# Attention plus mixture of experts on one core: one head pair turned on TensorE in fp32, and softmax inverse sums taken in pairs

## The chip, the cores and the metric

The kernel runs on one core of a Trainium2 chip, as one launch. The metric is the device time in microseconds (us) from start to end of the launch; lower is better. The engines are PE (matrix multiply, with PEld for its weight loads), DVE (vector), ACT (activation functions), POOL (GpSimd) and SP, whose queue here issues transfers and transposing transfers. Each engine takes its own instructions strictly in the order in which the program wrote them.

## The reference

Attention with rotary embedding over 4 batches, 8 heads, 576 positions and 64 dimensions, in fp32, then a layer of 8 experts that is applied densely with weights balanced by 8 Sinkhorn rounds:

```python
scores = (1 / np.sqrt(D)) * np.matmul(q_rot, k_rot.transpose(0, 1, 3, 2))
scores = scores - np.max(scores, axis=-1, keepdims=True)
attn = np.exp(scores)
attn = attn / (np.sum(attn, axis=-1, keepdims=True) + 1e-09)
x = np.matmul(attn, v)                  # regrouped to 2304 tokens x 512
P = np.exp(x @ w_gate - (x @ w_gate).max())
for _ in range(8):
    P /= P.sum(1, keepdims=True) + 1e-09
    P /= P.sum(0, keepdims=True) + 1e-09
    P *= N / E
for e in range(E):
    out += P[:, e:e + 1] * (np.maximum(x @ w1[e], 0.0) @ w2[e])
```

## The kernel before, in words

The 32 heads are taken as 16 pairs (p = 0 to 15, four to a batch). One pair needs 9 tiles of 128 queries: four per head, and one (u = 4) that holds 64 queries of each head. The tiles are numbered m = 9p + u. The steps of a tile, with the names that the order uses and the lines of the profile:

- `S`: scores on PE, an fp32 product (`s_mm`, L528). One S writes the tiles of both heads into a PSUM buffer; the program has three such double buffers (NS = 3).
- `M`: the row maximum, negated, on DVE (`m_max`, L532).
- `ex`: the exponential on ACT with its row sum (`e_exp`, L539). For u = 0, 2, 5, 7 it goes to an fp32 tile in SBUF, otherwise back into PSUM.
- `ei`: two DVE instructions on a 128x1 column, the sum plus 1e-9 (L545) and the reciprocal (L553), one pair of them for each tile.
- `eh`: exponential times inverse sum, rounded to fp16, on ACT (`e_hi`, L556). `el`: the rest, exponential times inverse sum minus eh, also as fp16, on DVE (`e_lo`, recorded at L414). For u = 7 ACT normalises (L559) and POOL subtracts (L563).
- `TR`: the tile's fp16 pair, 128x1152, is turned by a transposing transfer on the SP queue (`e_turn`, L605; u = 4 takes two).
- `AV`: the product with v on PE in fp16 (`av_mm`, L646): three terms, high and low part of v with the high part of the weights and the high part of v with the low part. v is split by `vh` (ACT, L418), `vl` (DVE, L414) and `vb` (DVE, L511).
- `h0, l0, h1, l1`: the result of each half of the queries to fp16 high and low parts of x (`x_half`, ACT L656, DVE L658).

Pairs 0 and 1 of a batch go one after the other. Pairs 2 and 3 of a batch are a group that shares the buffer of turned weights half by half (`GROUPS`, `split`), so their AV products come in column pieces of 256 and 32.

Beside the attention run the preparation of expert 0's weights (`wm`, `wz`, `wh`, `wl`) and, once x of enough pairs is there, its first product (`F1`, L783, three matmuls of 256 columns to a step), its evacuations (`Fh` on ACT L789, `Fl` on DVE L793), its second product (`F2`, L802) and the copies of its output (`Fo`, L807). After the last pair come the logits (`lm`, L668 and L673, and `le`, L681), the gate with its Sinkhorn rounds (`gate`, from L1021), sums of x for the experts to come (`xs`, L1100 to L1116 on DVE; `xp` on PE, L1140), the weights of the next half expert, and the scaling of expert 0's output (L1058). Then a second plan runs the remaining experts; its matmuls are all at L1312.

What comes when, up to the experts, is written out by hand: the string `ORDER` lists every step by name, and the program emits the instructions of all engines in that order. Semaphores are derived from the data and the buffers. So a step that waits holds up all that stands behind it on its engine.

```python
def e_inv(b):
    if not EIP:
        e_eps(b)
    t = b.pop()
    b.append(small.tile([P, 1], F32, tag="ei", bufs=12, name="ei"))
    dve.reciprocal(b[3], t)
```

Of the kernel before, what the change touches and what calls it, by code (L numbers as in the profile page):

```python
# [18 lines left out]
P = 128  # L19
# [12 lines left out]
GROUPS = tuple(g for b in range(4) for g in ((4 * b,), (4 * b + 1,), (4 * b + 2, 4 * b + 3)))  # L32
# [21 lines left out]
FLIP = ()  # L54
EIP = False
# [18 lines left out]
    PT=1.3, pa=0.75, pb=0.6,  # L74
# [16 lines left out]
et0.0 et1.0 ldv.0.0 ld.1 ldv.0.1 ly.1 w.1.0 w.2.0 ldv.0.2 w.1.1 ld.3 w.1.2 ldv.0.3 cq.1 ck.1 S.0.0 sq.1 M.0 v0.0  # L91
ex.0 aq.1 M.1 S.1.0 wm.1.0 ex.1 sk.1 ei.0 ei.1 ak.1 eh.0 v1.0 eh.1 M.3 M.2 ex.3 el.1 ex.2 el.0 ck.3 S.2.0 ei.2 TR.0
ei.3 eh.2 M.4 eh.3 el.2 ly.3 ex.4 el.3 ei.4 S.3.0 TR.3 wm.1.1 eh.4 el.4 M.5 TR.2 v2.0 sq.3 ex.5 M.6 S.4.0 ei.5 sk.3
ex.6 v3.0 eh.5 ld.2 M.7 ak.3 TR.1 ei.6 ex.7 vg.0 M.8 tt.v0 eh.6 ei.7 tm.v0 el.5 ex.8 ta.v0 el.6 vs.0 ck.2 S.5.0 TR.6
wm.1.2 vp.0 cq.3 w.1.3 ei.8 vh.0 M.10 TR.4 eh.7 vb1.0 M.9 eh.8 ex.9 el.8 ex.10 vl.0 S.6.0 TR.8 en.7 ei.10 ei.9 vb0.0
el.7 eh.9 TR.5 M.11 eh.10 M.12 ex.11 cq.2 el.10 TR.7 ex.12 wm.1.3 S.7.0 aq.3 ei.11 gx M.13 tt.g eh.11 AV.0.0.0 ly.2
ei.12 AV.0.0.1 ex.13 tm.g AV.0.0.2 AV.0.0.3 eh.12 ei.13 AV.0.0.4 el.11 ta.g eh.13 et0.1 TR.10 el.12 h0.0 gs S.8.0
TR.12 el.9 sk.2 l0.0 el.13 TR.9 M.14 sq.2 wx.1 wm.2.0 ex.14 tt.w1 AV.0.1.0 TR.11 AV.0.1.1 vh.1 aq.2 AV.0.1.2 M.15
S.9.0 ei.14 ex.15 vl.1 ak.2 eh.14 AV.0.1.3 ei.15 ld.4 M.16 AV.0.1.4 eh.15 et1.1 TR.13 M.17 ex.16 el.15 ex.17 ei.16
S.10.0 el.14 eh.16 tm.w1 en.16 w.2.1 ei.17 ta.w1 M.18 TR.14 eh.17 el.16 M.19 ex.18 el.17 ex.19 ei.18 S.11.0 vb1.1  # L100
eh.18 ei.19 TR.15 vb0.1 ws.1 eh.19 M.20 AV.1.0.0 wz.1.0 vh.2 AV.1.0.1 M.21 TR.17 AV.1.0.2 ex.20 AV.1.0.3 el.19
AV.1.0.4 wz.1.1 ex.21 et0.2 ei.20 S.12.0 ei.21 TR.16 eh.20 el.18 wz.1.2 eh.21 M.22 wh.1.0 TR.19 h1.0 el.21 ex.22
# [241 lines left out]
def attention_moe(ctx, tc, qk, v, trigs, eye, wg, w1, w2, out):  # L344
# [1305 lines left out]
```

## Time and profile before

| | us |
|---|---|
| three runs | 1641.42, 1639.41, 1638.05 |
| their median | 1639.41 |
| the profiled execution | 1643.98 |
| span of its trace, first to last instruction | 1642.2 |
| PE busy in the span | 1568.2 (95%) |
| DVE busy | 1378.7 (84%) |
| ACT busy | 1067.1 (65%) |
| POOL busy | 570.0 (35%) |

A sum over the trace is a sum against the profiled execution, which lies 1.78 us above its span and 4.57 us above the median. A busy PE includes the time in which the last columns of a matmul run out. PEclk, where it is printed, is the clock that TensorE was granted, as a share of 2.4 GHz; it knows two levels, 2.4 and 1.2 GHz, and a number between them is a mean over a stretch.

### The profile page before, as it was taken

How to read it: one execution, taken by the hardware profiler on the slowest of the kernel's cores; microseconds unless marked ns; L12 is line 12 of the kernel's file. 1: busy time of each engine (PE TensorE's matmuls, PEld its weight loads, DVE VectorE, ACT ScalarE, POOL GpSimd, SP SyncE). 2: the span in 40 equal slices, each digit the busy share in tenths (PEclk: the TensorE clock that was granted, in tenths of full speed). 3: DMA queues.
4: the chain of work that ended last, by engine and by line, in shares of the span. 5: the costliest groups of instructions: out<-in, count | busy, mean ns of one | idle time of the engine just before them, and what ended most of it. 6: DMA issues, size and time to landing. Idle time of an engine off the chain costs nothing.

```text
span 1642.2 us, 36750 instructions
## 1 busy us (share of the span) xinstructions
PE 1568.2 (95%) x14682; PEld 1305.4 (79%) x14682; DVE 1378.7 (84%) x2793; ACT 1067.1 (65%) x2192; POOL 570.0 (35%) x472
## 2 busy tenths in 40 slices
PE   4779999999889999999999999999999999999998
PEld 2446565666658989898989898989898989898987
DVE  7899898987869888888888888888888888888777
ACT  4778777874366766666666666666666666666642
POOL 4587444523123333333233323332333323232310
PEclk9879999999999999999999999999999999999999
DMA  8898999984224556565646464646464646464533
GB/s 255 166 195 174 191 189 204 184 141 107 78 102 123 149 129 156 126 158 124 160 121 163 119 165 116 167 114 170 112 171 111 168 116 163 121 161 123 133 100 97
DMA packets 226427, 238.99 MB, mean 146 GB/s; under 512 B 177360, under 2 KB 177488, under 8 KB 222672
## 3 DMA queue, kind: packets, MB, share of 16 engines
q1 hardware_dynamic: 207536, 175.30, 39.7%
q0 software_dynamic: 18720, 61.35, 20.9%
q8 instruction: 115, 1.88, 0.5%
q14 instruction: 56, 0.46, 0.1%
HBM read 123.36 MB, written 9.44 MB: 81 GB/s over the span
## 4 chain that ended last, share of the span: by engine, by line
PE 71%; DVE 4%; ACT 2%; issue 1%; DMA 0%; POOLq 0%; DVEq 0%; SPq 0%; ACTq 0%
PE m L1312 68%; PE g L783 1%; PE g L802 1%; ACT accA L1058 0%; PE g L646 0%; DMA wraw<-in_w 0%; DVE ts L1091 0%; DVE wmx L411 0%; DVE w1l L414 0%; DVE m L1104 0%; DVE hl L793 0%; DVE cs L1041 0%; DVE m L1100 0%; DVE ts L1149 0%; DVE w2l L414 0%
## 5 line engine op out<-in xcount | busy, mean ns | idle before, releaser
L1312 PE MATMUL m<-w2h,h 128*128 128x256 f16 x3528 | 627.2, 273 | 3.3 <-DVE accB L1375 1.5
L1312 PEld LDWEIGHTS <-h 128*128 128x128 f16 x5292 | 515.3, 98 | 63.5 <-issue 2.0
L1312 PE MATMUL m<-w2l,h 128*128 128x256 f16 x1764 | 480.8, 273 | 0.0
L1312 PEld LDWEIGHTS <-w1h 128*128 128x128 f16 x3920 | 369.2, 98 | 40.4 <-issue 3.7
L1312 PE MATMUL m<-ts,w1h 128*128 128x256 f16 (+1 forms) x2240 | 347.6, 262 | 1.9 <-ACT u L1335 1.3
L1377 ACT ACTIVATE ev<-m,pp 128x256 f32<-128x256 f32 x468 | 198.0, 469 | 186.1 <-PE m L1312 185.1
L1312 PE MATMUL m<-ts,w1l 128*128 128x256 f16 (+1 forms) x1120 | 284.0, 262 | 0.0
L1312 PE MATMUL m<-xx,w1h 128*128 128x256 f16 (+1 forms) x1680 | 261.4, 262 | 1.2 <-ACT accB L807 1.2
L1262 POOL TENSOR_TENSOR wraw<-wraw 128x512 f32<-128x512 f32 x112 | 159.2, 1421 | 185.0 <-issue 149.8
L1312 PE MATMUL m<-xx,w1l 128*128 128x256 f16 (+1 forms) x840 | 213.1, 262 | 0.0
L1312 PEld LDWEIGHTS <-w1l 128*128 128x128 f16 x1960 | 191.8, 98 | 17.7
L1357 POOL TENSOR_TENSOR h<-u,h 128x512 f16<-128x512 f32 (+1 forms) x70 | 78.2, 1117 | 362.1 <-ACT h L1353 362.1
L1375 DVE SCALAR_TENSOR_TENSOR ev<-m,pp,ev 128x256 f32<-128x256 f32 x351 | 154.8, 478 | 45.4 <-ACT ev L1377 28.3
L528 PE MATMUL s<-raw 64*128 64x288 f32 (+1 forms) x640 | 126.2, 480 | 39.8 <-DVE et L414 14.3
L1353 ACT ACTIVATE h<-m 128x512 f16<-128x512 f32 (+1 forms) x210 | 120.6, 574 | 44.1 <-PE m L1312 40.7
L1338 DVE TENSOR_TENSOR u<-m,u 128x512 f32<-128x512 f32 (+1 forms) x140 | 88.9, 635 | 55.0 <-PE m L1312 29.2
L528 PEld LDWEIGHTS s<-raw 64*128 64x128 f32 (+1 forms) x640 | 67.2, 197 | 83.9 <-issue 33.2
L1353 ACT ACTIVATE h<-u 128x512 f16<-128x512 f32 (+1 forms) x210 | 122.5, 587 | 14.8 <-DVE u L1364 11.1
L1335 ACT COPY u<-m 128x512 f32<-128x512 f32 (+1 forms) x140 | 76.0, 543 | 71.3 <-PE m L1312 70.3
L481 POOL TENSOR_TENSOR raw<-raw,trig 128x576 f32<-128x576 f32 x60 | 88.5, 1490 | 82.0 <-DMA raw<-in_qk 80.1
L532 DVE TENSOR_REDUCE nm<-s 128x1 f32<-128x576 f32 x144 | 105.4, 748 | 11.2 <-PE s L528 10.7
L1385 POOL DMA_DIRECT2D accA<-ev x78 | 69.2, 1021 | 126.4 <-ACT ev L1377 108.3
(159 smaller groups left out, 2735.7 us busy)
## 6 DMA issues: line engine op xcount, KB each, us to landing
ts<-xd SPq DMA_DIRECT2D x110, 512.0 KB, 3.9
accA<-ev POOLq DMA_DIRECT2D x78, 512.0 KB, 6.1
wraw<-in_w SPq DMA_DIRECT2D x28, 1024.0 KB, 4.9
raw<-in_qk SPq DMA_DIRECT2D x32, 576.0 KB, 4.7
accB<-ev POOLq DMA_DIRECT2D x26, 512.0 KB, 6.8
ts<-xd SPq DMA_DIRECT2D x28, 256.0 KB, 3.0
accB<-ev POOLq DMA_DIRECT2D x26, 256.0 KB, 3.3
vraw<-in_v SPq DMA_DIRECT2D x16, 320.0 KB, 5.0
```

Of the source, the lines that this page charges most:

```text
L481: engine[e].tensor_tensor(x, x, trig[:, n, :], op=ALU.mult)
L528: pe.matmul(o, q, x[r, 1, QH[kh]], start=True, stop=True)
L532: dve.tensor_reduce(b[0], ps[:, :, 0:HS], axis=AX.XY, op=ALU.max, negate=True)
L1262: put(k, "pool", US["ptt"], lambda: pool.tensor_tensor(quad(o), quad(x), quad(y), op=op), deps, uses=[raw])
L1312: pe.matmul(live[bank][:, f_ * width : (f_ + 1) * width], step(x, i, f_), y[:, i], start=first and f_ == 0 and n == 0, stop=n == 5, skip_g ...
L1335: act.copy(live[n], live[src])
L1338: dve.tensor_tensor(live[n], live[x], live[n], **add)
L1353: act.activation(t[:, 0:cols], live[src], func)
L1357: engine[eng].tensor_tensor(l, live[src], h, **sub)
L1375: dve.scalar_tensor_tensor(o, x, s, o, op0=ALU.mult, op1=ALU.add)
L1377: act.activation(o, x, AF.Copy, scale=s)
L1385: pool.dma_start(out=accs(th * NT2 + t0_, nt), in_=ev[th][:, 0:nt], accum_op=ALU.add)
```

## The change

Three things are done.

**Inverse sums in pairs.** The two tiles of one S write their row sums into the two columns of one 128x2 tile, and the two DVE instructions of `ei` run once for both, after both exponentials. The tail tile (u = 4) still has its own.

**Pair 3 by another way** (`WHOLE = (3,)`). Its exponentials stay whole in fp32, in SBUF tiles borrowed from the pool of expert 0's hidden layer (`e_whole`). ACT makes a 128x128 diagonal of each tile's inverse sums (`dg`, `e_diag`). PE multiplies the exponentials, as weights, with that diagonal in fp32, which turns and normalises them at once into a PSUM buffer of the scores' kind (`PT`, `e_flip`). ACT copies the result into storage inside x that is not yet in use (`tc`, `e_copy`), and the product with v runs in fp32 on the unsplit v. So pair 3 has no `eh`, `el`, `TR`, `vh`, `vl` and `vb`. Pair 2 stands alone, and its AV products come in pieces of 288 columns.

**The order.** The string is written anew, the part after the last pair too. The steps of pair 3 stand between those of pairs 1 and 2. One unused cast of the identity at the start (`idf`, L1537) is gone, and unused functions for turning fp16 on PE.

```diff
-GROUPS = tuple(g for b in range(4) for g in ((4 * b,), (4 * b + 1,), (4 * b + 2, 4 * b + 3)))
+WHOLE = (3,)
+GROUPS = ((0,), (1,), (2,)) + tuple(g for b in range(1, 4) for g in ((4 * b,), (4 * b + 1,), (4 * b + 2, 4 * b + 3)))
+ND = 3
...
+    turned = xx.bitcast(F32).rearrange("p a c h n -> p (a c) h n")
+    last64 = att.tile([P, S], F32, name="last64")
...
+    def e_inv(two, n):
+        t, r = (small.tile([P, n], F32, tag=x, bufs=k, name=x) for x, k in (("et", 8), ("ei", 12)))
+        dve.tensor_scalar(t, two[0], 1e-9, 2.0**-N_TOP, op0=ALU.add, op1=ALU.mult)
+        dve.reciprocal(r, t)
+        two.append(r)
...
+    def e_whole(ps, b, n, two, j, k):
+        if not two:
+            two.append(small.tile([P, k], F32, tag="es", bufs=8, name="es"))
+        t = ("hh", "hl")[n % 2]
+        b += [two, hA.tile([P, 2048], F16, tag=t, bufs=2, name=t)[:, 0 : 2 * S].bitcast(F32), j]
+        act.activation(b[2].rearrange("p (a b) -> p a b", a=2), ps[:, :, 0:HS], AF.Exp, bias=b[0], accum_out=two[0][:, j : j + 1])
+
+    def e_diag(b):
+        b.append(att.tile([P, P], F32, tag="dg", bufs=ND, name="dg"))
+        act.activation(b[4], ident, AF.Copy, scale=inv(b))
+
+    def e_flip(bs, j):
+        t = ps_s.tile([P, 2, 512], F32, tag="s", name="s").rearrange("p a b -> p (a b)")
+        bs[j].append(t)
+        mm = lambda *x: pe.matmul(*x, start=True, stop=True)
+        x, d = bs[j][2], bs[j][4]
...
+        for k in range(4):
+            mm(t[:, k * P : k * P + P], x[:, k * P : k * P + P], d)
+        for h, r in enumerate(HEADS if j else ()):
+            mm(t[r, 512:640], bs[h][2][:, 512:576], bs[h][4])
+
+    def e_copy(n, bs, j):
...
+        copy(turned[:, 4 * j : 4 * j + 4, h, HS + q : HS + q + P], t[:, 0:512].rearrange("p (k w) -> p k w", k=4))
+        if j:
+            copy(last64[:, QT[i] : QT[i] + P], t[:, 512:640])
...
     def av_mm(p, qh, jt):
...
+        if p in WHOLE:
+            b, c = divmod(p, KC)
+            for j, r in enumerate(HEADS):
+                k, y = (slice(0, P), turned[:, 4 * j + jt, qh, HS:]) if jt < 4 else (r, last64[r, QH[qh]])
+                pe.matmul(po[r], vraw[b][k, c, j, jt, :], y, start=jt == 0, stop=jt == 4)
+            return
```

Where the instructions move, by engine. First DVE from the first row maximum of pair 0: `L532` and, in the changed kernel, `L531` is M, `L411` and `L406` are maxima of v and of weights, `L414` and `L409` is el. Before:

```order
L532 TENSOR_REDUCE nm<-s 128x1
L411 TENSOR_REDUCE wmx<-wraw 128x1
L545 TENSOR_SCALAR et<-es 128x1
L553 RECIPROCAL ei<-et 128x1
L545 TENSOR_SCALAR et<-es 128x1
L553 RECIPROCAL ei<-et 128x1
L411 TENSOR_REDUCE vmx<-vraw 128x1
L532 TENSOR_REDUCE nm<-s 128x1 x2
```

And now:

```order
L531 TENSOR_REDUCE nm<-s 128x1 x2
L406 TENSOR_REDUCE wmx<-wraw 128x1
L543 TENSOR_SCALAR et<-es 128x2
L544 RECIPROCAL ei<-et 128x2
L406 TENSOR_REDUCE vmx<-vraw 128x1
L531 TENSOR_REDUCE nm<-s 128x1 x2
```

Four small instructions between two pairs of maxima became two, on two columns.

Then PE in the middle of pair 3, between scores of pairs 2, 3 and 4: `L527` is S, `L564` is PT (an x4 row is four fp32 products; the rows of 64 are the last 64 positions), `L659` is AV of pair 3 in fp32, `L857` and `L864` are the turn of a maximum of weights. All rows but S are new:

```order
L564 MATMUL s<-dg,hh 128x128 x4
L564 MATMUL s<-dg,hl 128x128 x4
L564 MATMUL s<-dg,hh 64x128
L564 MATMUL s<-dg,hl 64x128
L527 MATMUL s<-raw 128x288 x4
L659 MATMUL g<-xx,vraw 64x288 x4
L659 MATMUL g<-last_106,vraw 64x288 x2
L564 MATMUL s<-dg,hl 128x128 x4
L564 MATMUL s<-dg,hh 64x128
L564 MATMUL s<-dg,hl 64x128
L564 MATMUL s<-dg,hh 128x128 x4
```

The fp32 products of pair 3 stand between scores, and each group of PT rows takes one of the PSUM buffers of the scores; before, the products of pair 3 with v stood later, in pieces of 256 and 32 columns, and no product turned anything.

Last DVE behind the last logits (`L681`, `L682` and now `L706`, `L707`): `L1100` to `L1116` and now `L1137` are sums of x, `L793` and `L818` is Fl, `L1021`, `L1022` and now `L1058`, `L1059` open the gate. Before:

```order
L681 COPY lg<-g 128x2x24
L682 TENSOR_TENSOR lg<-g,lg 128x2x24
L1100 TENSOR_TENSOR m_5505<-xx 128x512
L1104 TENSOR_TENSOR m_5505<-m_5505,c_5506 128x512
L1106 TENSOR_TENSOR u_5507<-xx,m_5505 128x512
L793 SCALAR_TENSOR_TENSOR hl<-g,hh 128x256
L1109 TENSOR_TENSOR u_5507<-u_5507,xx 128x512
L1091 TENSOR_TENSOR ts<-m_5505,ts 128x512
L1112 TENSOR_TENSOR u_5508<-xx,u_5507 128x512
L1116 TENSOR_TENSOR u_5508<-u_5508,xx 128x512
L1091 TENSOR_TENSOR ts<-u_5507,ts 128x512
L793 SCALAR_TENSOR_TENSOR hl<-g,hh 128x256
```

And now:

```order
L706 COPY lg<-g 128x2x24
L707 TENSOR_TENSOR lg<-g,lg 128x2x24
L1058 TENSOR_SCALAR lg<-lg,inv 128x144
L1059 TENSOR_TENSOR lg<-lg,ctok 128x144
L1061 TENSOR_REDUCE gmx<-lg 128x1
L818 SCALAR_TENSOR_TENSOR hl<-g,hh 128x256
L1137 TENSOR_TENSOR m_5057<-xx 128x512
L818 SCALAR_TENSOR_TENSOR hl<-g,hh 128x256
```

The gate, which stood behind a block's sums of x and two Fl, now opens directly behind the logits. Behind that place stand 86 steps of F1 where there were 70, and 22 of Fl where there were 18; the 56 steps of F2 are the same.

## Rows read from the trace of the kernel before

**Rows 1.** Windows: us, busy PE, PEld, DVE, ACT, POOL, clock, DMA share.

```profile
0.00:20.00 20.00, 5.53 (x16) 3.02 (x16) 12.23 (x19) 4.15 (x8) 9.42 (x12) 1.00 0.79 286
20.00:110.00 90.00, 62.25 (x384) 36.74 (x384) 81.01 (x185) 62.88 (x128) 56.19 (x40) 0.81 0.89 195
110.00:200.00 90.00, 82.69 (x783) 54.47 (x782) 80.39 (x185) 69.71 (x153) 62.16 (x44) 0.96 0.87 177
200.00:300.00 100.00, 97.24 (x924) 61.61 (x924) 88.59 (x211) 77.35 (x166) 49.55 (x35) 1.00 1.01 199
300.00:391.00 91.00, 88.58 (x959) 62.03 (x956) 70.57 (x175) 65.14 (x142) 25.14 (x20) 1.00 0.89 153
391.00:498.00 107.00, 93.05 (x626) 60.55 (x625) 86.48 (x182) 52.31 (x104) 28.88 (x22) 1.00 0.23 84
498.00:1642.00 1144.00, 1138.92 (x11002) 1026.95 (x11002) 959.47 (x1842) 735.60 (x1495) 338.71 (x303) 1.00 0.54 137
```

**Rows 2.** Chain that ended last, in order of time: start, us, what.

```profile
360.50 0.17 DVE et L545
...
360.77 1.40 DVE nm L532 x2
...
378.65 2.08 PE g L646 x56
...
390.88 0.22 DVE lg L681
...
400.96 1.11 DVE lg L1021
...
475.21 4.90 ACT accA L1058 x8
...
497.93 1116.11 PE m L1312 x10756
```

**Rows 3.** Waits of PE, 0 to 200 us: engine, line, releaser, us, times, longest.

```profile
PE s L528 <- DVE et L414: 13.7, 7, 3.6
...
PE s L528 <- ACT e L539: 10.2, 8, 1.9
```

**Rows 4.** DVE and ACT groups, 0 to 500 us: busy, mean ns, idle before.

```profile
L414 DVE SCALAR_TENSOR_TENSOR et<-s,ei,et 128x576 f16<-128x576 f32 x80 | 65.0, 812 | 10.2 <-ACT et L556 9.7
L556 ACT ACTIVATE et<-s,ei 128x576 f16<-128x576 f32 x80 | 58.7, 736 | 15.9 <-DVE ei L553 10.3 <-ACT s L539 2.6 <-issue 1.3
...
L414 DVE SCALAR_TENSOR_TENSOR et<-e,ei,et 128x576 f16<-128x576 f32 x48 | 48.3, 1006 | 1.6 <-ACT et L556 1.6
...
L553 DVE RECIPROCAL ei<-et 128x1 f32<-128x1 f32 x144 | 23.6, 164 | 4.9
...
L545 DVE TENSOR_SCALAR et<-es 128x1 f32<-128x1 f32 x144 | 21.1, 146 | 10.8 <-ACT s L539 7.9 <-ACT e L539 2.3
...
L414 DVE SCALAR_TENSOR_TENSOR vl<-vraw,s,vh 128x640 f16<-128x640 f32 x16 | 14.7, 920 | 0.0
...
L511 DVE COPY vb<-vh 64x512 f16<-64x512 f16 x32 | 12.3, 385 | 0.9
...
L1146 ACT CAST ts<-x 128x256 f16<-128x256 f32 x4 | 1.5, 367 | 3.1 <-PE x L1140 3.1
```

**Rows 5.** PE in order of time, 204 to 208 and 417 to 419 us.

```profile
204.86 2.36 PE L528 MATMUL s<-raw 64*128 64x288 f32 x16
...
418.00 0.51 PE L1037 MATMUL g<-prob,ones 128*128 128x144 f32 x2
418.37 0.38 PE L783 MATMUL g<-xx,wh 128*128 128x256 f16 x2
418.58 0.27 PE L783 MATMUL g<-xx,wl 128*128 128x256 f16 x1
```

**Rows 6.** Weight loads by form, 0 to 500 us: busy, mean ns.

```profile
L783 PEld LDWEIGHTS <-wh 128*128 128x128 f16 x576 | 53.9, 99 | 29.4 <-issue 14.7 <-DVE hl L793 2.3 <-DVE xx L658 0.5
...
L1037 PEld LDWEIGHTS g<-prob,ones 128*128 128x128 f32 x16 | 2.6, 189 | 1.9 <-DVE prob L1034 1.6
```

More of the change, by code (lines that the diff above doesn't have):

```diff
@@ L457, in v_scale @@
         vs[b] = s, inv
+        if any(p // KC == b for p in WHOLE):
+            xscale[b] = small.tile([P, 1], F32, tag="xs", name="xs")
+            dve.tensor_single_scalar(xscale[b], s, 2.0 ** -(N_TOP + 12), op=ALU.mult)
     def v_ctok(b):
@@ L532, in m_max, with e_exp @@
         dve.tensor_reduce(b[0], ps[:, :, 0:HS], axis=AX.XY, op=ALU.max, negate=True)
[L534 to L535 removed]
+    def e_exp(ps, b, out, two, j, n):
+        if not two:
+            two.append(small.tile([P, n], F32, tag="es", bufs=8, name="es"))
         e = ps[:, :, 0:HS]
[L537 to L541 removed]
@@ L543, in e_eps @@
-    def e_eps(b):
-        t = small.tile([P, 1], F32, tag="et", bufs=8, name="et")
-        (pool if EIP else dve).tensor_scalar(t, b[1], 1e-9, 2.0**-N_TOP, op0=ALU.add, op1=ALU.mult)
-        b.append(t)
-    def e_inv(b):
-        if not EIP:
-            e_eps(b)
-        t = b.pop()
-        b.append(small.tile([P, 1], F32, tag="ei", bufs=12, name="ei"))
-        dve.reciprocal(b[3], t)
+        t = att.tile([P, 2, HS], F32, tag="e32", bufs=E32, name="e32") if out else e
+        act.activation(t, e, AF.Exp, bias=b[0], accum_out=two[0][:, j : j + 1])
@@ L588, in attention_moe @@
     place = {m: i for i, m in enumerate(SEQ)}
+    for p in WHOLE:
+        GROUP_OF[p] = (p,)
+        for h in range(2):
+            first[p, h] = 9 * p + 5 * h
+        before.update({5 * p + i: 5 * p + i - 1 for i in range(1, 5)})
     def et(n):
@@ L814, in attention_moe @@
     plan = Plan(dict(
[L815 removed]
+        rx=ZB, ry=RY, e32=E32, S=NS, G=NG, E=NEB, W=4, dg=ND, ET0=1, ET1=1, vraw=1, vhl=NVV, hA=2, raw0=3, tail=NTAIL,
         H=2, stg=1, X=4, ts=3,
@@ L877, in pair_ops @@
                 )
-            for j in range(1 if i == TAIL else 2):
-                u, bb = 2 * i + j - (i > TAIL), []
+            js, two = range(1 if i == TAIL else 2), []
+            bs, pts = [[] for _ in js], [("S", (n, j)) if 2 * i + j - (i > TAIL) not in EU else ("e32", 9 * p + 2 * i + j - (i > TAIL)) for j in js]
+            for j in js:
+                u, bb = 2 * i + j - (i > TAIL), bs[j]
                 m = 9 * p + u
```

402 lines of the change are left out of this document (198 added, 204 removed).

## The prediction

> **What bounds the kernel now.** I read the windows first, with edges at the stages [rows 1]. From 498 us on PE is busy for 1138.92 of 1144 us, and the chain that ended last shows it as one piece of 1116.11 us at L1312 [rows 2]. The change touches nothing there, so it can only move the moment at which that piece begins. Ahead of it lie three stages, and the same rows tell what each is short of. From 20 to 200 us DVE is busy for 161.40 of 180 us (90%; sums of the two rows), PE for 144.94 (81%) and ACT for 132.59 (74%); the granted clock averages 0.81 until 110 us, so PE spent part of this at its 1.2 GHz level. From 200 to 391 us PE is busy for 185.82 of 191 us (97%), DVE for 159.16. From 391 to 498 us neither is full: PE 93.05 and DVE 86.48 of 107 us.
>
> The waits say the same of the first stage: PE's scores wait 13.7 us on `el` and 10.2 us on exponentials [rows 3], so there DVE and ACT hold up PE. After 200 us PE's 97% says that it is the limit itself.
>
> **DVE.** There are 144 pairs of small instructions now, 23.6 + 21.1 us busy, 0.31 us each [rows 4]. Back to back they lie closer: in the chain 0.27 us go by from the start of one such pair to the next maximum [rows 2]. The change leaves 80 pairs, five for each of 16 head pairs. A column more I cost at nothing, since their 0.16 us are for one element per partition. So 64 x 0.27 = 17.3 us go (64 x 0.31 = 19.8 at most); of these half, 8.6 us, before 200 us, taking the first 8 of 16 pairs to lie there. Pair 3 loses 8 `el`: five at 0.812 and three at 1.006 us make 7.1 us. Its `vl` (0.92 us) and two `vb` (2 x 0.385 us) make 1.7 us [rows 4]. In all DVE has 26.1 us less, 17.4 of them before 200 us. The unused cast stands ahead of 20 us, where DVE is busy for 12.23 of 20 us only [rows 1]; I leave it out.
>
> **ACT.** Pair 3 loses nine `eh` (0.736 us each), one normalisation of the same size and a `vh` (its counterpart on DVE takes 0.92 us): 8.3 us. It gains nine copies of 512 columns (the tail's three pieces count as one), four of 128 and nine diagonals of 128 columns. ACT takes 0.736 us for 576 columns and 0.367 for 256 [rows 4]; on that line 512 columns come to 0.66 us and 128 to 0.22, an estimate: 9 x 0.66 + 13 x 0.22 = 8.8 us. ACT comes out even.
>
> **PE.** PT is 46 fp32 products, which the trace records as two passes each. The nearest row is the gate's fp32 product of 144 columns [rows 5]: its two passes fill 0.51 us, and the next matmul starts 0.37 us after the first pass. That is 0.19 us a pass from outside. At the other end, a pass of 288 columns in S costs 0.29 us beside a second one on the other half of the rows (2.36 us for 16), which by columns would leave 0.13 us for 128. So 92 passes cost between 92 x 0.13 = 12 and 92 x 0.19 = 17 us; I take 13 us, near the lower end, because the gate's row is a single product with nothing of its own behind it. AV of pair 3 is 20 products, 40 passes of 288 columns, two heads side by side on the output's halves: 20 x 0.29 = 5.9 us, or 11.7 us if the heads do not run together. The fp16 products that it replaces took 2 x 2.08 = 4.2 us [rows 2]; pair 2 without pieces saves some tenths, 0.3 us. PE gains 13 + 5.9 - 4.5 = 14.4 us (13.4 to 24).
>
> The trace has a sign that fp32 weights are the dear part: a load of 128 fp32 columns takes 189 ns, one of fp16 99 [rows 6]. The Trainium skill, page "TensorE: Matmul & The Clock Gate", section "Weight-path perf modes — Fast Weight Load (FWL) and DoubleRow", says that the fast load is not used for FP32 weights, and the two rows agree with it; by that rule a pass of 128 columns would go at the pace of its load, 92 x 0.189 = 17.4 us in place of 13, and the sum below would be 4 us worse.
>
> **POOL and SP.** POOL loses one subtraction, SP ten of its transposing transfers (nine tiles, the tail twice) in a stage with a DMA share of 0.87 to 0.89 [rows 1]. Neither engine holds up the stage by the waits above; I count nothing, and if that is wrong it is a gain.
>
> **The waits that are added.** `ei` now waits for the second exponential too, so the first tile's `eh` can start up to one exponential (0.74 us by the size of `eh`) later, and a tile in PSUM is held that long. Behind it on DVE stand the next maxima, and for the buffer waits S. It is hidden where ACT does the second exponential at once anyway; where not, it is a rival below. PT waits for a diagonal from ACT, and behind PT on PE stands the next S.
>
> **The sum, by stages.** From 20 to 200 us: if DVE stays the limit at its 90%, 17.4 us less of it end the stage 19 us sooner. But PE then needs 144.9 + 14.4 = 159.3 us: at the share it reached from 110 to 200 us (82.69 of 90, 92%) that is 173 us, 7 us sooner; at the 97% of the next stage 164 us, 16 us sooner. PE is the tighter one, and I take the middle, **11 us**. From 200 to 391 us PE is the limit and only what leaves its list counts: 16 more steps of F1 now stand behind the last logits. They are 48 matmuls of 256 columns, two of which take 0.21 us where they follow each other (418.37 to 418.58) [rows 5]; that is **5 us**. The rest of DVE's relief here (8.6 us) is hidden by PE. From 391 to 498 us these 5 us come back on PE, and four `Fl` on DVE, none longer than an `el` of 0.812 us, 3 us: at most 8 us; against it the gate's first step, which started 10.1 us behind the logits (390.88 to 400.96) [rows 2], opens at once. The scaling of expert 0's output waits for the gate and started at 475.21 us; so up to 10 us could be gained. Between -10 and +8 I take **+2 us**. In all 11 + 5 - 2 = 14 us: 1643.98 - 14 = 1630 us for an execution like the profiled one. That one lies 4.6 us above the median of the three runs, so against the median the forecast is **1625 us**.
>
> **The rivals.**
> *DVE alone decides.* If PE takes pair 3 in its idle time without any queueing, the first stage ends 19 us sooner, the second gains DVE's 8.6 us, the third loses 2: 26 us, 1613 us. For it: PE has 35 us idle between 20 and 200 us, and a denser PE might keep the 2.4 GHz level. Against it: the 97% after 200 us.
> *The fp32 loads are not hidden, slower.* Place: PE's list between pairs 1 and 4, up to some 110 us. If each PT pass pays load and columns one after the other, 0.189 + 0.13 = 0.32 us, PT costs 29 us, AV without side by side 11.7, and PE has 29 + 11.7 - 4.5 = 36 us more: 181 us at 97% take 186 us, 6 us over the 180. With -5 and +8 that is 9 us more, 1648 us. It decides from about 27 us of extra work (a pass at 0.22 us): then the first stage gains too little to pay for the third. Against it: fp16 loads of 99 ns vanish beside matmuls that follow at 0.21 us for two [rows 5, 6]. The Trainium skill, same page, Part 3 "What overlaps and what doesn't", has loads run beside matmuls only in other rows of the array, which speaks for this rival; the fp16 rows here do not agree with it.
> *The paired inverse sums hold the buffers.* If half of the 32 double tiles before 200 us show 0.74 us of the wait, 12 us, the first stage gains nothing; what is left is -5 + 2, so 1636 us, at the edge of what can be told from 1639. For it: S already waits on exponentials. Against it: the written order puts both exponentials in a row.
>
> **How the numbers follow.** My forecast has a chance of 0.56, its own range 1613 to 1633 (PE's two ends in the first stage, 7 and 16 us, and the third from -5 to +6). DVE alone: 0.18. Loads not hidden: 0.14. Held buffers: 0.12. From no change a measurement can tell about 0.2%, 3.3 us, which is also the spread of the three runs. Faster: the forecast, DVE alone and a sixth of the held buffers, 0.76. Same: the other held buffers, 0.10. Slower: 0.14. The range 1606 to 1641 takes in the DVE end with 7 of the 10 us that the third stage could give, and the held buffers; it leaves out the slow rival.
>
> **What would show it.** Right: two small instructions per S in place of four, PE above 88% busy from 20 to 190 us where DVE is below it, the logits' evacuation near 375 us in place of 390.88, the long L1312 piece beginning near 484 us. PT passes near 0.14 us. Wrong: PT spread over 20 us or more; PE waits on diagonals or exponentials grown beyond the 24 us of [rows 3]; the long piece beginning at 498 us although the logits came sooner, which would put the loss into the third stage; a lower clock from 60 to 110 us.

## The result, and the profile after

The changed kernel takes **1650.10 us** (median of 4 runs, 1648.14 to 1652.51) against 1639.45 us for the kernel before: a ratio of 1.0071, 95% interval 1.0057 to 1.0084. It is 0.7% slower, beyond the range of the forecast. The profiled execution took 1651.78 us, its span 1650.0 us.

The windows after, with the edges and columns of [rows 1]:

```profile
0.00:20.00 20.00, 5.53 (x16) 3.02 (x16) 10.28 (x17) 4.95 (x9) 7.43 (x11) 1.00 0.74 267
20.00:110.00 90.00, 66.41 (x411) 41.60 (x412) 74.68 (x146) 62.91 (x142) 57.47 (x42) 0.92 0.80 184
110.00:200.00 90.00, 80.29 (x701) 52.16 (x701) 83.01 (x156) 68.89 (x151) 60.84 (x46) 0.96 0.83 177
200.00:300.00 100.00, 93.49 (x900) 60.26 (x899) 86.88 (x163) 73.74 (x162) 45.35 (x33) 0.98 0.80 178
300.00:391.00 91.00, 88.36 (x843) 57.84 (x843) 72.62 (x147) 64.45 (x140) 21.17 (x16) 1.00 0.77 152
```

Up to 391 us the busy time of DVE adds up to 327.5 us, against 332.8 in [rows 1]. The forecast took 26.1 us from DVE; 5.3 went, although 68 instructions fewer stand between 20 and 200 us (146 and 156, where [rows 1] has 185 and 185). PE has 146.7 us from 20 to 200 us, 1.8 more than before, so its idle time was not filled, and its scores wait as long as before (from 0 to 200 us; columns of [rows 3]):

```profile
PE s L527 <- DVE et L409: 15.5, 10, 4.1
...
PE s L527 <- ACT e L538: 7.6, 5, 2.9
```

That is 23.1 us where [rows 3] has 23.9.

The chain that ended last, after (start, us, what), against [rows 2]:

```profile
395.32 0.22 DVE lg L706
...
482.86 4.90 ACT accA L1095 x8
...
505.56 1116.11 PE m L1349 x10756
```

The logits come out 4.4 us later than in [rows 2] (395.32, 390.88) where 375 was forecast, and the long expert piece begins 7.6 us later (505.56, 497.93). So 4.4 us are lost ahead of the logits and 3.2 behind them. Where the first 4.4 lie, the first row maximum of pair 8 tells. It is the 73rd of 144 in both kernels, behind all those of pairs 0 to 7; first the kernel before, then the changed one:

```profile
200.04 0.74 DVE L532 TENSOR_REDUCE nm<-s 128x1 f32<-128x576 f32 x1
...
198.87 0.74 DVE L531 TENSOR_REDUCE nm<-s 128x1 f32<-128x576 f32 x1
```

The first stage ends 1.2 us sooner, where 11 were forecast. From there to the logits it takes 196.5 us in place of 190.8, where 5 us less were forecast. (Behind this place the new order has four steps of F2 and two of AV more, so the cut between the stages is rough by these.) One row of DVE's groups shows what was not expected (busy us, mean ns, idle before):

```profile
L543 DVE TENSOR_SCALAR et<-es 128x2 f32<-128x2 f32 x64 | 32.3, 505 | 12.4 <-ACT s L538 9.9 <-ACT hh L555 1.1 <-ACT hl L555 0.6
...
L544 DVE RECIPROCAL ei<-et 128x2 f32<-128x2 f32 x64 | 10.6, 166 | 2.2
L544 DVE RECIPROCAL ei<-et 128x1 f32<-128x1 f32 x16 | 2.6, 164 | 0.5
...
L543 DVE TENSOR_SCALAR et<-es 128x1 f32<-128x1 f32 x16 | 2.4, 150 | 0.9 <-ACT s L538 0.8
```

The paired reciprocal costs what one column cost (166 and 164 ns). The paired scaling does not: 505 ns on average, 32.3 us in all, more than the 21.1 us that the 144 single ones took [rows 4]. Its sixteen unpaired neighbours on the same line stay at 150 ns. The timeline of the longest one, GpSimd beside it (start, us, engine, line):

```profile
112.94 1.56 POOL L746 TENSOR_SCALAR wraw<-wraw,s 128x512 f32<-128x512 f32 x1
...
114.47 1.56 POOL L484 TENSOR_TENSOR raw<-raw 128x576 f32<-128x576 f32 x1
114.68 1.37 DVE L543 TENSOR_SCALAR et<-es 128x2 f32<-128x2 f32 x1
115.98 1.40 POOL L480 TENSOR_TENSOR raw<-raw,trig 128x576 f32<-128x576 f32 x1
116.08 0.17 DVE L544 RECIPROCAL ei<-et 128x2 f32<-128x2 f32 x1
```

The scaling starts 0.21 us after a GpSimd instruction and ends at 116.05, 0.02 us after that one has ended. Sorted this way, 35 of the 64 start while a GpSimd instruction runs and take 0.786 us on average (up to 1.37); 29 start beside none and take 0.165 (up to 0.171). All that take more than 0.2 us, 33, are among the first, and 30 of them end 0.02 to 0.03 us after the GpSimd instruction beside which they started. (The expectation of by columns below was written with 33 and 31, at 0.815 and 0.174 us; the trace has the counts given here.) That is the first theory, **P**: the two-column form needs something of GpSimd's and waits for it. The rivals were **O**, the new written order and the third stage cost the time, and **H**, the paired wait holds buffers, the third rival of the prediction.

### The profile page after: what moved, and what is told of

Its sections match the earlier page's. It is cut to its first block, busy times and chain, and to the rows that moved or that the text cites. A ratio compares the mean times of both kernels' runs of the same rounds, so it can differ in the third digit from the quotient of the medians.

```text
span 1650.0 us, 36526 instructions
## 1 busy us (share of the span) xinstructions
PE 1577.3 (96%) x14646; PEld 1311.7 (79%) x14646; DVE 1377.9 (84%) x2654; ACT 1065.2 (65%) x2205; POOL 562.4 (34%) x471
## 4 chain that ended last, share of the span: by engine, by line
PE 72%; DVE 4%; ACT 1%; issue 1%; DMA 0%; SPq 0%; POOLq 0%; DVEq 0%; ACTq 0%
PE m L1349 68%; PE g L827 2%; PE g L808 1%; PE g L670 1%; ACT accA L1095 0%; PE s L527 0%; DVE hl L818 0%; DVE w1l L409 0%; DMA wraw<-in_w 0%; DVE w2l L409 0%; DVE et L409 0%; DVE ts L1186 0%; DVE prob L1080 0%; DVE ts L1128 0%; DMA ET<-et 0%
## 5 line engine op out<-in xcount | busy, mean ns | idle before, releaser
L1349 PEld LDWEIGHTS <-w1l 128*128 128x128 f16 x1960 | 191.8, 98 | 17.8
L527 PE MATMUL s<-raw 64*128 64x288 f32 (+1 forms) x640 | 122.4, 469 | 40.3 <-DVE et L409 16.5
L1375 DVE TENSOR_TENSOR u<-m,u 128x512 f32<-128x512 f32 (+1 forms) x140 | 88.9, 635 | 54.9 <-PE m L1349 29.2
L1390 ACT ACTIVATE h<-u 128x512 f16<-128x512 f32 (+1 forms) x210 | 122.3, 586 | 14.8 <-DVE u L1401 11.1
L527 PEld LDWEIGHTS s<-raw 64*128 64x128 f32 (+1 forms) x640 | 66.1, 194 | 81.1 <-issue 31.7
L531 DVE TENSOR_REDUCE nm<-s 128x1 f32<-128x576 f32 x144 | 103.7, 748 | 14.5 <-PE s L527 14.0
L480 POOL TENSOR_TENSOR raw<-raw,trig 128x576 f32<-128x576 f32 x60 | 84.8, 1427 | 77.6 <-DMA raw<-in_qk 77.6
```

The costliest lines, as they stand in the source:

```text
L480: engine[e].tensor_tensor(x, x, trig[:, n, :], op=ALU.mult)
L527: pe.matmul(o, q, x[r, 1, QH[kh]], start=True, stop=True)
L531: dve.tensor_reduce(b[0], ps[:, :, 0:HS], axis=AX.XY, op=ALU.max, negate=True)
L1349: pe.matmul(live[bank][:, f_ * width : (f_ + 1) * width], step(x, i, f_), y[:, i], start=first and f_ == 0 and n == 0, stop=n == 5, skip_g ...
L1375: dve.tensor_tensor(live[n], live[x], live[n], **add)
L1390: act.activation(t[:, 0:cols], live[src], func)
```

## The experiments

Times are medians; ratios are to the kernel before, run beside each, whose median lay between 1638.54 and 1641.13 us. The kernel before was run with its profile once more:

> The kernel before once more, unchanged, for a second profiled execution: the first lay 4.6 us above the median of its runs, and its granted clock from 80 to 110 us was 0.65, where every kernel with pair 3 in fp32 has 0.89 to 0.99. If the lower clock belongs to the kernel, it is below 0.8 there again and the logits are out at 388 to 392 us; if it was that execution's, the clock is higher, the logits are out 3 to 6 us earlier, and that much of the gain that the experiments' profiles show against [rows 1] is none.

1640.38 us against 1641.13 (0.9975 to 1.0013). Its profiled execution took 1644.40 us, again 4 us above the median, with the logits out at 391.54 us and a clock of 0.68 from 80 to 110 us. So the clock belongs to the kernel, but both profiled executions of it lie some 4 us high, and gains read between two profiles against [rows 1] are some us too large. Where in the span these 4 us lie is not known. Below, the verdicts go by the ratios.

| kernel | median us | ratio, 95% interval | logits out, us |
|---|---|---|---|
| changed | 1650.10 | 1.0071, 1.0057 to 1.0084 | 395.32 |
| by columns | 1641.77 | 1.0009, 1.0000 to 1.0019 | 385.33 |
| unpaired | 1643.52 | 1.0025, 1.0014 to 1.0036 | 387.44 |
| scaling on ACT | 1637.33 | 0.9983, 0.9974 to 0.9993 | 378.70 |
| no inverse | 1632.44 | 0.9954, 0.9937 to 0.9971 | 377.27 |
| PT twice | 1641.30 | 1.0015, 1.0002 to 1.0028 | 384.01 |
| DVE dose | 1641.82 | 1.0007, 0.9996 to 1.0018 | 384.65 |
| DVE dose, double | 1645.26 | 1.0042, 1.0030 to 1.0054 | 388.52 |
| port dose | 1650.81 | 1.0061, 1.0041 to 1.0082 | 394.35 |
| ACT dose | 1641.16 | 1.0007, 0.9998 to 1.0017 | 385.12 |
| before: pairing alone | 1668.07 | 1.0173, 1.0158 to 1.0187 | 414.95 |
| before: pairing by column | 1651.25 | 1.0075, 1.0059 to 1.0091 | 397.97 |

**By columns: the width of the scaling alone.**

```diff
-        dve.tensor_scalar(t, two[0], 1e-9, 2.0**-N_TOP, ...)
+        for c in range(n):
+            dve.tensor_scalar(t[:, c : c + 1], two[0][:, c : c + 1], 1e-9, 2.0**-N_TOP, ...)
```

> The changed kernel with one edit: the scaling of the two sums is written as two instructions of one column (128x1) in place of one of 128x2; the reciprocal stays paired, order and all else stay. Theory P (the 128x2 form shares something with GpSimd: of 64 such instructions 33 began while a GpSimd instruction ran and took 0.815 us on average, 31 began without one and took 0.174): no scaling takes longer than 0.2 us; 33 x 0.66 = 22 us of busy DVE go, 64 x 0.147 = 9.4 us come, about 12 us less DVE up to the logits, half of it before 200 us; the logits are out 4 to 9 us earlier and the time is 1641 to 1646 us. Rival O (the new written order and the third stage cost it): the long scalings go, but the time stays within 3 us of 1650. Rival H (the paired wait holds the buffers): the time stays within 3 us of 1650, since the pairing is untouched.

Measured 1641.77 us, inside P's range; 8.3 us below the changed kernel, whose interval it does not touch. Its row on DVE:

```profile
L544 DVE TENSOR_SCALAR et<-es 128x1 f32<-128x1 f32 x144 | 17.8, 146 | 10.4 <-ACT s L538 7.5 <-ACT e L538 0.8 <-ACT hh L556 0.7
...
L545 DVE RECIPROCAL ei<-et 128x2 f32<-128x2 f32 x64 | 10.6, 166 | 2.2
```

80 instructions became 144, and the busy time fell from 34.7 to 17.8 us, more than the 12 us expected; the logits are out 10.0 us earlier, where 4 to 9 were. O and H, which left the time at 1650, fall as causes of these 8 us.

**The form by itself.** A kernel that runs each form 16 times beside an idle GpSimd and again beside a busy one:

> A kernel of its own that leaves out the whole computation: on DVE 16 instructions each of the scaling of 1, 2 and 4 columns in SBUF, of 2 columns read from PSUM, of the reciprocal of 2 columns and of a scalar_tensor_tensor of 2 columns with two SBUF inputs; once with GpSimd idle and once beside a run of GpSimd multiplications. Theory P: with GpSimd idle all lie between 0.06 and 0.25 us; beside GpSimd the scalings of 2 and 4 columns in SBUF and the two-input form take a GpSimd instruction each (about 1 us or more), while the scaling of one column, that from PSUM and the reciprocal stay as they were. If it were the number of columns alone, the form from PSUM and the reciprocal would be long too; if GpSimd had no part in it, nothing would change between the two halves.

Its groups; the lines up to L47 have GpSimd idle, those from L54 on have it multiplying:

```profile
L58 DVE TENSOR_SCALAR b<-src 128x4 f32<-128x4 f32 x16 | 10.9, 762 | 0.0
L64 DVE SCALAR_TENSOR_TENSOR bs<-src 128x2 f32<-128x2 f32 x16 | 10.2, 709 | 0.0
L56 DVE TENSOR_SCALAR b<-src 128x2 f32<-128x2 f32 x16 | 10.0, 705 | 0.0
...
L47 DVE SCALAR_TENSOR_TENSOR as<-src 128x2 f32<-128x2 f32 x16 | 1.2, 150 | 0.0
L39 DVE TENSOR_SCALAR a<-src 128x2 f32<-128x2 f32 x16 | 1.2, 158 | 0.0
L43 DVE TENSOR_SCALAR ap<-pss 128x2 f32<-128x2 f32 x16 | 1.1, 146 | 0.0
L60 DVE TENSOR_SCALAR bp<-pss 128x2 f32<-128x2 f32 x16 | 1.1, 143 | 0.0
L45 DVE RECIPROCAL ar<-src 128x2 f32<-128x2 f32 x16 | 1.1, 141 | 0.0
L62 DVE RECIPROCAL br<-src 128x2 f32<-128x2 f32 x16 | 1.1, 139 | 0.0
L37 DVE TENSOR_SCALAR a<-src 128x1 f32<-128x1 f32 x16 | 1.1, 143 | 0.0
L54 DVE TENSOR_SCALAR b<-src 128x1 f32<-128x1 f32 x16 | 1.0, 138 | 0.0
```

The scaling of two columns in SBUF goes from 158 to 705 ns beside GpSimd (L39, L56). One column does not (143, 138), two columns read from PSUM do not (146, 143), and neither does the reciprocal of two columns (141, 139). So it is not the number of columns: it is this operation from SBUF to SBUF with more than one. P stands. The mean of 705 ns mixes two kinds: from the third instruction on, one takes 1.37 us and the next one 0.155, in turn. One of the long ones:

```profile
17.64 1.37 DVE L56 TENSOR_SCALAR b<-src 128x2 f32<-128x2 f32 x1
```

So every second one waits for about one GpSimd instruction (1396 ns each), where the expectation had all of them wait. The form with two SBUF inputs waits as well (L47, L64: 150 and 709 ns). The kernel before has it in the subtractions from `e32`, 1006 ns beside 812 for those from PSUM [rows 4]: 20 of the 48 start while a GpSimd instruction runs and take 1.28 us on average, the other 28 take 0.81, and those from PSUM take 0.81 either way. That pair of rows was in front of the forecast and was not read as a wait.

The Trainium skill, page "SBUF — State Buffer", section "Who interferes with whom", says that a tensor_scalar in a two-port mode contends with GpSimd for a pair of ports which whoever came first keeps for its whole instruction, and that two SBUF inputs contend with a GpSimd instruction that reads SBUF; these rows agree on both. That the two columns put the scaling in such a mode no row shows by itself.

**The pairing alone, in the old order.** Here `WHOLE = ()`, the old `GROUPS` and the old `ORDER` return, one `ei` per double tile stands where the second stood, and the steps that need it move behind it:

> The kernel before with the pairing alone: one 128x2 scaling and one 128x2 reciprocal per double tile, put where the second of the two stood (what depends on it follows as soon as it may); head pair 3 is worked as before, and so is the rest of the order. Theory P: about half of the 64 scalings wait for GpSimd, 22 us, against 64 x 0.27 = 17 us saved: 1639 to 1647 us, with scalings over 0.5 us in the trace. Rival O: 1630 to 1638, since the old order is back. Rival H: 1645 or more, by the longer hold.

> As the pairing alone, with the scaling written by columns: two of 128x1 and one reciprocal of 128x2 per double tile. Theory P: no long scalings, 64 reciprocals (10 us) less than the kernel before, some of it gained: 1632 to 1640 us, and at least 3 us below the run with the 128x2 scaling. Rival O: equal to that run within 2 us, both at 1630 to 1638. Rival H: equal to it within 2 us, both at 1645 or more.

1668.07 and 1651.25 us: 1.7% and 0.75% slower than before, and both above what P alone gave. The difference of 16.8 us is P's again; the scalings of the first:

```profile
L558 DVE TENSOR_SCALAR et<-es 128x2 f32<-128x2 f32 x64 | 25.7, 401 | 29.2 <-ACT s L553 27.8 <-ACT e L553 1.2
```

They lie with 401 ns below the changed kernel's 505, and yet cost more. The rest, 11 us over the kernel before with 64 reciprocals fewer, speaks for a cost of the paired wait in this order, which was not made for pairs: `ei` waits 27.8 us for the second exponential here, 9.9 us in the changed kernel. That it comes by held buffers, as H has it, is not shown: PE's scores wait 23.7 us for subtractions and exponentials from 20 to 200 us in the pairing by column, and 22.7 in the kernel before.

**Unpaired, in the new order.** Each tile gets its own scaling and reciprocal again; the rest is the changed kernel:

```diff
-                    plan.add(f"ei.{first}", ..., lambda two=two, k=len(js): e_inv(two, k), [f"ex.{m - i}" for i in js], uses=pts)
+                    plan.add(f"ei.{m}", ..., lambda own=own: e_inv(own, 1), [f"ex.{m}"], uses=[p2])
```

> The changed kernel with the inverse sums unpaired again, as in the kernel before: every tile has a scaling and a reciprocal of 128x1 of its own; the first of a double tile stands behind the DVE instruction that follows the double tile's second maximum, the second where the pair's stood. Head pair 3 on PE and the rest of the written order stay. Against the run by columns (1641.8 us) it has 64 reciprocals more on DVE, 64 x 0.166 = 10.6 us, and no wait for the second exponential. Theory D (the amount of work on DVE decides the first stage): 1643 to 1650 us. Theory H (the wait of the paired form decides, since a first tile's sum and its PSUM buffer wait for the second exponential): 1630 to 1639 us. If both cancel: 1639 to 1643.

1643.52 us: at the lower edge of theory D (the amount of work on DVE decides), half a microsecond above "both cancel", and not H. In this order pairing by columns is worth 1.0025 - 1.0009 = 0.16%, 2.6 us, though it saves 10.6 us of reciprocals. If a microsecond of DVE is worth no more than one of the time, the added wait costs at most the rest, 8 us. Pair 3 on PE and the new order without any pairing cost 0.25%.

**Whose work sets the pace?** Four runs:

> The changed kernel with the scaling of the sums by 2 to the -14 taken from DVE: ACT does it on two columns at once, right behind the second exponential, without the 1e-9 (the sums are at least 1, where 1e-9 changes no bit); DVE keeps the paired reciprocal. DVE loses the 17.8 us of scalings of the run by columns, ACT gains 80 instructions of some 0.2 us, 16 us. Theory D: 1630 to 1638 us. Theory H: no better than by columns, 1640 to 1648, since ACT's instruction lengthens the way from the exponential to the reciprocal.

> The run by columns with each fp32 product of PT issued twice, the second overwriting the first with the same values: 92 passes more, about 16 us of PE between 60 and 100 us. If PE is the tighter engine of the first stage, as the prediction had it: 10 to 16 us more, 1652 to 1658. If PE has idle time there that takes it: within 4 us of 1642. If the sum of the prediction was too low on PT by a factor, the row shows it: a pass over 0.19 us.

> The changed kernel without the inverse sums: the scaling and the reciprocal are left out and a fixed scale stands in their place, so the probabilities are not normalised; all else stays. It is the most that any saving on this step could bring: DVE has 31 us less than by columns (17.8 + 13.2), and nothing waits for a second exponential or an inverse. Theories D and H: 1615 to 1628 us, with the logits out at 360 to 372 us. If neither the work nor the wait of this step sets the pace (PE's own work, loads or the buffers do): 1634 us or more.

> The kernel before with one part of it moved: the scaling of the sums (144 of 128x1, 21.1 us on DVE) is done by ACT behind each exponential, without the 1e-9; nothing is paired, pair 3 and the order are as before. DVE has 21 us less, ACT 144 x 0.2 = 29 us more. At the price that the runs so far give to DVE's work (from by columns to no inverse 31 us of DVE were worth 9.4 us of time, to ACT's scaling 17.8 us were worth 4.5, about 0.3 us each): 1631 to 1637 us if ACT's work costs nothing; 1638 to 1645 if ACT's is worth as much as DVE's.

The scaling on ACT: 1637.33 us, in D's range and below both kernels, by 0.17% of the one before (0.07 to 0.26%), about the least a measurement can tell. The 80 instructions cost ACT 203 ns each, as expected. PT twice: 1641.30. PE is busy with PT for 21.5 us there and for 13.5 in by columns, so 8 us more work of PE cost nothing that can be told (the expectation had 16 us). Without any inverse sums: 1632.44, above the 1615 to 1628 of D and H, so the forecast's 1625 was out of reach in this order for **any** saving on this step. The same move to ACT in the kernel before: 1646.44 (1.0035, 1.0022 to 1.0047), above both ranges and slower, though DVE had 21 us less to do; but ACT had 29.2 us more, and the reciprocals waited 25.0 us for it. So a saving on DVE is not worth the same in every order.

**Is it the PSUM buffers?** `EU = (0, 2, 4, 5, 7)` in place of `(0, 2, 5, 7)`, on two bases:

> The run by columns with one constant changed: the fifth tile of a pair (64 rows of each head) also has its exponentials written to SBUF, as tiles 0, 2, 5 and 7 have, so its PSUM buffer is free after the exponential and not after the subtraction. Theory B (what is left of the first stage's waits is the way through three PSUM buffers, scores, maximum, exponential, inverse, scaling, subtraction, and not the amount of work of an engine): the waits of the scores for the subtraction fall from 14.8 us (20 to 200 us, by columns) to under 10, and the time to 1633 to 1639 us. Otherwise: 1640 us or more, since this tile's subtraction reads SBUF and takes 0.94 in place of 0.81 us.

> The run with the scaling on ACT (1637.3 us) with the same constant changed. Theory B: 1629 to 1635 us. Otherwise 1636 us or more.

1643.19 (1.0025, 1.0015 to 1.0035) and 1640.17 us (0.9999, 0.9988 to 1.0010): no faster than their bases, by the ratios 0.16% slower each. PE's waits for the subtraction fell only from 14.8 to 12.2 us, and those for exponentials rose from 5.5 to 8.7. Theory B falls in this form.

**Doses.** Work that nobody reads, behind the reciprocal of by columns (the ACT dose: behind the exponential):

```diff
         dve.reciprocal(r, t)
+        y = small.tile([P, n], F32, tag="jk", bufs=8, name="jk")
+        for c in range(n):
+            dve.tensor_scalar(y[:, c : c + 1], two[0][:, c : c + 1], ...)
```

The double dose runs that loop twice; the port dose has `dve.tensor_scalar(y, two[0], ...)` in its place.

> The run by columns with its 144 scalings of 128x1 issued a second time, behind the reciprocal, into a tile that nobody reads: 144 x 0.147 = 21 us more of DVE, on no way that anything waits for but DVE's queue. If DVE's work sets the pace: 1652 to 1663 us (0.5 to 1 us each). At the price of the runs so far, 0.25 to 0.3: 1645 to 1650. If only the delay to the inverse counts: within 2 of 1641.8.

> The run by columns with 80 scalings more in the paired form (64 of 128x2, 16 of 128x1), behind the reciprocal, into a tile that nobody reads: some 30 us more busy time of DVE, most of it waiting for GpSimd. If the port wait costs as time of DVE's queue: 1648 to 1658 us, 8 us or more over by columns, as in the changed kernel. If it costs by delaying the inverse: within 4 of 1641.8. GpSimd's own instructions show whether they are held up in turn.

> The run by columns with ACT's scaling of the sums issued behind each second exponential, as in the run with the scaling on ACT, but into a tile that nobody reads: 80 x 0.2 = 16 us more of ACT, DVE unchanged. If ACT's work counts as DVE's does: 1645 to 1652 us, and then taking the scaling from DVE was worth that much more than the 4.5 us seen. If ACT's work is hidden: within 2 of 1641.8.

> The run by columns with its scalings of 128x1 issued twice more behind the reciprocal, into a tile that nobody reads: 288 x 0.138 = 29 to 40 us more of DVE, four pieces, 0.55 us, per double tile, where the port dose had 0.47 on average in one piece of 0.14 to 1.4 us. If the amount of DVE's work is what the port wait costs: 1648 to 1655 us, as with the port dose. If the long pieces are: within 3 of 1641.8.

The rows of the added work: DVE dose, double dose, port dose.

```profile
L548 DVE TENSOR_SCALAR jk<-es 128x1 f32<-128x1 f32 x144 | 14.6, 138 | 0.0
```

```profile
L548 DVE TENSOR_SCALAR jk<-es 128x1 f32<-128x1 f32 x288 | 29.1, 144 | 0.6
```

```profile
L547 DVE TENSOR_SCALAR jk<-es 128x2 f32<-128x2 f32 x64 | 30.2, 472 | 0.0
```

14.6 us of DVE in pieces of 0.14 us cost nothing (1641.82 us; 1.0007). 16 us of ACT cost nothing (1641.16). 30.2 us of scalings that wait for GpSimd cost 9.0 us (1650.81, 1.0061), as in the changed kernel, although no scaling of exponentials waits for them: so the wait costs as time of DVE's queue, and a delay of the inverse is not needed for it. 29.1 us in small pieces cost 0.33% over by columns, 5.4 us (1645.26, 1.0042), more than the 3 us that the theory of the long pieces allowed and less than the amount should. The intervals of double dose and port dose overlap, so the shares of the amount and of the long pieces are not settled.

## Why the prediction was wrong

- **The step that failed first is "A column more I cost at nothing, since their 0.16 us are for one element per partition".** It holds for the reciprocal (166 ns) and not for the scaling (505 ns). The two instructions of `ei` took 44.7 us before [rows 4] and take 47.9 now (32.3 + 10.6 + 2.6 + 2.4): 3.2 us more, where 17.3 less were forecast. So the relief of 26.1 us became 5.3 us up to 391 us. By columns, which has the rest of the change, gives back 8.3 of the 10.7 us by which the changed kernel is slower (by the ratios 0.62 of 0.71%). None of the three rivals had this mechanism. The slower one came out at 1648 us, near the 1650 measured, and that is chance: it put its price on PT, which was to cost 29 us and is busy for 13.4.
- **"If DVE stays the limit at its 90%, 17.4 us less of it end the stage 19 us sooner" failed too.** A busy time of 90% was not a limit. Up to its logits by columns has 17.6 us of DVE less than the kernel before, two thirds of the relief forecast, and takes as long (1.0009); first the kernel before, then by columns:

```profile
0.00:390.88 390.88, 336.16 (x3056) 217.77 (x3057) 332.67 (x771) 279.23 (x594) 202.34 (x148) 0.95 0.91 187
...
0.00:385.33 385.33, 335.10 (x2972) 218.61 (x2973) 315.04 (x691) 275.99 (x603) 196.19 (x147) 0.98 0.83 183
```

  31 us less than by columns were worth 9.3 us, 14.6 us more nothing. The DVE dose's windows show 327.3 us of DVE up to 391 us, the changed kernel's 327.5, and their medians lie 8.3 us apart. A queue that is 90% busy by the windows had room for 14.6 us of small pieces, and not for 30.2 us with waits of up to 1.4 us. The windows count these waits as busy, so the share by itself could not tell work from waiting.
- **"PE is the tighter one" failed**, and with it the 11 us: the share of 92 to 97% that I let PE reach over the whole stage was not there to be had. The stage was read as one stretch of 180 us. Cut into 30 us, the kernel before has PE busy for

```profile
20.00:50.00 30.00, 20.36 (x81) 10.48 (x82) 26.39 (x62) 19.86 (x42) 14.52 (x11) 1.00 0.89 209
50.00:80.00 30.00, 21.67 (x142) 13.19 (x141) 25.72 (x63) 19.78 (x41) 17.77 (x12) 0.77 0.79 166
80.00:110.00 30.00, 20.22 (x162) 13.07 (x162) 28.90 (x63) 23.24 (x47) 23.89 (x18) 0.65 0.99 209
```

  and the kernel without inverse sums

```profile
20.00:50.00 30.00, 20.41 (x88) 11.34 (x90) 27.13 (x43) 18.88 (x40) 17.71 (x14) 1.00 0.94 204
50.00:80.00 30.00, 24.54 (x174) 16.74 (x170) 22.71 (x37) 24.43 (x57) 16.14 (x12) 0.83 0.79 170
80.00:110.00 30.00, 26.16 (x185) 16.32 (x184) 20.55 (x33) 21.82 (x51) 28.71 (x21) 0.89 0.87 210
```

  Of the 35 us that PE idles from 20 to 200 us, 9.6 lie before 50 us and stayed there (9.6) even without the step that the change was to shorten. From 50 to 110 us the idle time fell from 18.1 to 9.3 us; by the medians this kernel, which saves the most of all, is 7 us faster than the one before.
- **"From 200 to 391 us PE is the limit and only what leaves its list counts" failed too, and with it the 5 us.** The row maximum that opens pair 8 comes at 193.56 us in by columns and at 189.65 without inverse sums:

```profile
193.56 0.74 DVE L531 TENSOR_REDUCE nm<-s 128x1 f32<-128x576 f32 x1
...
189.65 0.76 DVE L533 TENSOR_REDUCE nm<-s 128x1 f32<-128x576 f32 x1 [1.01 <-PE s L529]
```

  From it to the logits it takes 190.8 us in the kernel before, 196.5 in the changed one, 191.8 in by columns and 187.6 without inverse sums. The last three have the same order and the same work on PE there (184.3 us busy both in by columns and without inverse sums); only `ei` on DVE, and what waits for it, differs. So PE's share of 97% did not make it the limit, and the rest of DVE's relief was not hidden by PE. Of the 11 us of the first stage by columns got 6.5, against a profile of the kernel before that lies some 4 us high.
- **The costs of PE's new work were right.** Eight PT passes fill 1.16 us, 0.145 each, where I took 0.14, and PT is busy for 13.4 us in all, where I took 13 (the first sixteen passes, from 67.3 us, took 3.6 us, 0.23 each; the granted clock was 0.56 from 66 to 71.3 us). A pass of 0.32 us, the rival "the fp32 loads are not hidden", is not seen. AV of pair 3 is busy for 7.4 us, between the 5.9 and 11.7 given:

```profile
75.34 1.16 PE L564 MATMUL s<-dg,hh 128*128 128x128 f32 x8
```

```profile
L659 PE MATMUL g<-xx,vraw 128*64 128x288 f32 x32 | 6.0, 525 | 0.0
...
L659 PE MATMUL g<-last,vraw 64*64 64x288 f32 x8 | 1.4, 428 | 0.0
```

  PT was spread over 30 us (67 to 97 us), which I had named as a sign of a wrong forecast. PT twice says that PE's time for it costs nothing that can be told; what the spread itself cost, no run tells.
- **The third stage was right:** +2 us forecast, 110.2 us after in place of 107.1, and 108.7 to 111.6 in every run with the new order.
- **The held buffers** (0.12): pairing by column costs 11 us in the old order, and in the new one the added wait costs at most 8 us, by the estimate above, where what pairing saves outweighs it. That buffers are the reason is not shown.

What set the pace of the first stage in the place of busy engines is not settled. Added work on PE (8 us), ACT (16 us) and DVE (14.6 us in small pieces) cost nothing each, and an earlier release of one PSUM tile did not help. What fits all of it is that the engines wait for each other in a written order, so that a delay counts where it stands; that is argued, not shown. No hold-up of GpSimd in turn shows: its instructions on L484 take 1450 ns, their counterparts in the kernel before 1464, and in the kernel of forms GpSimd takes 1396 ns beside L56 and 1388 when DVE is done.

## What to carry to other kernels

Before two small instructions are made one, ask whether the wider form waits for another engine where the narrow one does not: here two columns of fp32 from SBUF to SBUF wait for GpSimd and one does not, and the one instruction takes 505 ns where the two took 292. Where the same operation shows two durations by the place of its operands, as 1006 and 812 ns did, look at what runs beside it. And before a share of 90% or 97% busy is trusted as a limit, try it with a dose of work that nobody reads, or take work from another engine and see whether the stage gets shorter.

## What the runs showed of the hardware

- Two fp32 columns SBUF to SBUF through a tensor_scalar: 158 ns alone, 705 beside GpSimd, up to 1.37 us in the kernel; one column, a PSUM source and a reciprocal are free of it.
- With more work on PE the granted clock from 80 to 110 us was higher: 0.65 and 0.68 in two executions of the kernel before with PE busy for 20.2 and 19.6 us, 0.94 after with 25.5, and 0.99 with PT twice and 27.2 us. It does not follow the busy time alone: without inverse sums it was 0.89 with 26.2. That a part of the added work was paid by time at the 2.4 GHz level is argued from these rows, not shown.
- The eight weight loads of the PT passes at 75.34 us show 191 ns each, like the 189 of [rows 6], and fill 1.0 us; the passes follow each other at 0.145 us. So these loads overlap. The 218 ns of the longest group are a mean over two levels of the clock: the first eight of them, from 67.3 us, show 327. The row of 75.2 to 76.3 us, and that of the longest group:

```profile
L564 PEld LDWEIGHTS s<-dg,hh 128*128 128x128 f32 x8 | 1.0, 191 | 0.2 <-issue 0.2
...
L564 PEld LDWEIGHTS s<-dg,hl 128*128 128x128 f32 x40 | 5.7, 218 | 4.4 <-ACT dg L559 1.6 <-ACT hl L555 1.4 <-ACT xx L681 0.8
```
